# Attention batch by batch, with half steps of the feed-forward layer between its units

## The chip, the cores and the metric

The kernel runs on one core of one Trainium2 chip. The metric is the device time of one execution in microseconds; the kernel before took 638.37 us (median of 3 runs, 638.03 to 641.25). PE is TensorE, DVE VectorE, ACT ScalarE, POOL GpSimd and SP SyncE, which issues the transfers here.

## The reference, cut

Decaying linear attention over 2 batches, 8 heads, 768 tokens and head dimension 64, then two feed-forward layers over the 1536 tokens with a model dimension of 512: the first 2048 wide with a piecewise quadratic, the second 1536 wide and gated.

```python
for b in range(nb):                                   # blocks of 64 tokens
    intra = np.einsum('bhij,bhjd->bhid', np.einsum('bhic,bhjc->bhij', qb, kb) * Dmask, vb)
    inter = np.einsum('bhid,bhde->bhie', qb * lam_pow, kv_state)
    out[:, :, sl] = intra + inter
    kv_state = lam_block * kv_state + np.einsum('bhsd,bhse->bhde', kb * rev_pow, vb)
x = out.transpose(0, 2, 1, 3).reshape(B * S, H * D)
h = x @ w_in                                          # moe
x = np.where(h >= 1, h, np.where(h <= -1, 0, (h + 1) ** 2 / 4)) @ w_out
gate = 1 / (1 + np.exp(-(x @ w_gate)))                # moe2
return (gate * (x @ w_val)) @ w_out2
```

## The kernel before, in words

**Attention** goes in 16 units of 384 tokens: a batch `b`, a pair of heads `p` and a half `h` of the sequence, three chunks of 128 tokens each. The loop over `i` writes out by hand, in program order on every engine, a software pipeline: for the next unit `scores(i + 1)` and `updates(i + 1)` on PE, then `weigh_states(i + 1)` (DVE weighs the scores by the table `DT` into `pT`, L320, and adds up the states `sc`, L329 and L331; ACT copies them into the block-diagonal `st`, L343); for the unit after that `pre(i + 2)` on POOL (decayed keys `kd`, L262, and queries `qs`, L272); for this unit `outputs(i)` on PE (L354, L363) and `evacuate(i)` (ACT rounds into `xh`, L373, DVE forms the rest `xl`, L374). Then SP loads unit `i + 4` (`u_load`, four buffers) and, in most units, a piece of weights (`w_load`). The order of units is pair by pair, and within a pair batch 0 and then batch 1. The first pair's tables are made on chip; those of the other pairs go through a small tensor in DRAM (`pd`) and come back as `DT[:, 2:]` (L250) and `qp[:, 1:]` (L245). `kd` and `qs` have three buffers each.

**Weights** are float64 and come in 68 pieces of 512 columns. A weight round (`w_round`) takes three neighbouring pieces one step further each: two ACT operations take the words of piece `k` apart (`w_words`, L77, L78), two DVE operations and one on DVE or POOL make the float of piece `k - 1` (`w_float`, L84, L85, L87), ACT rounds piece `k - 2` into its high half (`w_high`, L91), and DVE or POOL forms its low half (`w_low`, L95). A piece is thus ready three rounds after its first step. Between units, rounds use POOL and stand at units 2, 4, 6, 8, 10, 12, 13, 14 and 15. There are 18 buffers for ready pieces and 6 for raw ones; a round is put off while its buffer still holds a hidden slice in use (`prog["done"]`).

**The feed-forward layers** work in steps: for a hidden slice of 128 and a token tile of 512, `hidden` (12 matmuls of 512 columns, L136 to L138; 24 in the second layer), the split of the previous step's activation into `gh` (ACT, L420) and `gl` (DVE, L421), the activation of this step, and `project` of the step before the previous one (12 matmuls, L466), a lag of two. Four slices make a group that accumulates in four PSUM banks, which `flush` adds up in SBUF. Three token tiles run inside a group. `act1` of the first layer is a relu on ACT (L428), a min and multiplication on DVE (L429), and a max on DVE (L430). One round of weights follows a step of the first layer (none behind a flush), two a step of the second. Only the very first `hidden` (`early`) is issued inside the last attention unit. PSUM is split into a pool of five banks (scores, updates, projections) and one of three (outputs, hidden).

Of the kernel before, what the change touches and what calls it, by code (L numbers as in the profile page):

```python
# [33 lines left out]
def fused_kernel(ctx: ExitStack, tc: tile.TileContext, qkv, qd, cst, w1, w2, out):  # L34
# [62 lines left out]
    # One round takes each of three pieces a step further, so that no engine waits  # L97
    # for another.
# [33 lines left out]
    def three(ps, pairs):  # L132
        """ps += A.B over pairs of split operands, without the product of the two rests."""
        n = len(pairs)
        for j, ((ah, al), (bh, bl)) in enumerate(pairs):
            pe.matmul(ps, lhsT=ah, rhs=bh, start=(j == 0), stop=False)  # L136
            pe.matmul(ps, lhsT=al, rhs=bh, start=False, stop=False)  # L137
            pe.matmul(ps, lhsT=ah, rhs=bl, start=False, stop=(j == n - 1))  # L138

    def hidden(n, t, o):  # L140
        w_need(n, o)
        ps = ps_h.tile([P, TT], F32, tag="h", name=f"h{n}_{t}_{o}")
        tt = slice(t * TT, (t + 1) * TT)
        three(ps, [(w_at(n, o + k * P), (xh[:, k, tt], xl[:, k, tt])) for k in range(NP)])
        return ps

    first = []

    def early():
        first.append(hidden(0, 0, 0))  # L150

# [1 line left out]
    with ExitStack() as actx:  # L153
# [5 lines left out]
        units = [(b, p, h) for p in range(NP) for b in range(B) for h in range(NHALF)]  # L159
# [24 lines left out]
        pw = kp.tile([H, 2 * P], F32, name="pw")  # L184
        pd = dp.tile([H, 2 * P], F32, name="pd")

        # States of a pair's heads, and the same as diagonal blocks
# [3 lines left out]
        def tables():  # L191
            # The first pair's, by doubling from the anti-diagonal.
# [19 lines left out]
            for j in range(2):  # L212
                dve.memset(dm[j][:, :, 0:PADW], 0.0)
            pool.memset(pw[:, 0:P - 1], 0.0)
# [20 lines left out]
            # The others by way of DRAM, from the powers: column x of pw holds lam^(x - 127), or 0.  # L235
# [22 lines left out]
        def pre_k(i):  # L258
            """Keys by what is left of their decay at the chunk's end."""
            b, p, h = units[i]  # L260
            kd[i] = sp2.tile([P, CU, 2, D], F32, tag="kd", bufs=3, name=f"kd{i}")
            pool.tensor_tensor(  # L262
                out=kd[i], in0=raw_u[i][:, 2].rearrange("p (c h d) -> p c h d", c=CU, h=2),
                in1=DT[:, 2 * p:2 * p + 2, P - 1:P].unsqueeze(1).to_broadcast([P, CU, 2, D]),
                op=ALU.mult,
            )

        def pre_q(i):
            """Queries by the decay since the chunk's start."""
            b, p, h = units[i]  # L270
            qs[i] = sp2.tile([P, CU, P], F32, tag="qs", bufs=3, name=f"qs{i}")
# [9 lines left out]
        def scores(i):  # L281
            u = raw_u[i]
            S_ps[i] = []
            for e in range(2):
                s = ps_a.tile([P, 512], F32, tag="a", name=f"s{i}_{e}")
                S_ps[i].append(s)
# [25 lines left out]
        def weigh_states(i):  # L312
# [3 lines left out]
            sb, sd = sc[(p * B + b) % 2], st[(p * B + b) % 2]  # L316
# [28 lines left out]
        def outputs(i):  # L345
            b, p, h = units[i]
            u = raw_u.pop(i)
            sb = st[(p * B + b) % 2]
            xb = ps_h.tile([P, TT], F32, tag="h", name=f"x{i}")
            x = xb[:, 0:UT]  # L350
# [28 lines left out]
        with tc.manual_schedule():  # L379
# [8 lines left out]
            pre_q(1)  # L388
            for i in range(nu):
# [5 lines left out]
                else:  # L395
                    early()
# [16 lines left out]
    acp = ctx.enter_context(tc.tile_pool(name="acp", bufs=1, reuse_waits="tile"))  # L413
    gp = ctx.enter_context(tc.tile_pool(name="gp", bufs=2, reuse_waits="tile"))
    part = acp.tile([P, NTT * 4, 512], F32, name="part")

    def parts(g, n, t):
        gh = gp.tile([P, TT], F32R, tag="gh", bufs=3, name=f"gh{n}_{t}")
        gl = gp.tile([P, TT], F32R, tag="gl", bufs=3, name=f"gl{n}_{t}")
        act.activation(gh, g, AF.Copy)  # L420
        dve.tensor_tensor(out=gl, in0=g, in1=gh.bitcast(F32), op=ALU.subtract)  # L421
        return gh, gl

    def act1(ps, n, t):
        """(h + 1)^2 / 4 between -1 and 1, 0 below, h above."""
        r = gp.tile([P, TT], F32, tag="r", name=f"r{n}_{t}")
        g = gp.tile([P, TT], F32, tag="g", name=f"g{n}_{t}")
        act.activation(r, ps, AF.Relu, bias=half, scale=0.5)  # L428
        dve.scalar_tensor_tensor(out=r, in0=r, scalar=1.0, in1=r, op0=ALU.min, op1=ALU.mult)  # L429
        dve.tensor_tensor(out=g, in0=r, in1=ps, op=ALU.max)  # L430
        return g

    def act2(ps, pv, n, t):
        r = gp.tile([P, TT], F32, tag="r", name=f"r{n}_{t}")
        g = gp.tile([P, TT], F32, tag="g", name=f"g{n}_{t}")
        act.activation(r, ps, AF.Sigmoid)  # L436
        dve.tensor_tensor(out=g, in0=r, in1=pv, op=ALU.mult)  # L437
        return g

    half = acp.tile([P, 1], F32, name="half")  # L440
    seq = []
    for ph, nf in ((0, NF1), (1, NF2)):
        for g in range(nf // GF):
            for t in range(NTT):
                for f in range(GF):
                    seq.append((ph, g, t, f))

    accs = {}

    def project(u, gs):  # L450
        ph, g, t, f = u
        gh, gl = gs
        n = ph * NF1 + g * GF + f
        o = (512, 1024)[ph]
        w_need(n, o)
        w = ws[index[n, o]]
        for j in range(4):
            if f == 0:
                accs[j] = ps_a.tile([P, 512], F32, tag="a", name=f"a{ph}_{g}_{t}_{j}")
            js = slice(j * P, (j + 1) * P)  # L460
            if ph == 0:
                ops = [(w[:, 0, js], gh), (w[:, 1, js], gh), (w[:, 0, js], gl)]
            else:
                ops = [(gh[:, js], w[:, 0]), (gh[:, js], w[:, 1]), (gl[:, js], w[:, 0])]
            for m, (a, b_) in enumerate(ops):
                pe.matmul(accs[j], lhsT=a, rhs=b_, start=(f == 0 and m == 0),  # L466
                          stop=(f == GF - 1 and m == 2))

# [122 lines left out]
```

## Time and profile before

| what | value |
|---|---|
| median of 3 runs | 638.37 us (638.03 to 641.25) |
| span of the profiled execution | 637.2 us |
| its own device time | not given apart; the span is 1.2 us under the median |
| PE, DVE, ACT, POOL busy | 97%, 61%, 40%, 10% of the span |
| mean granted TensorE clock | 0.994 |

The profile is one execution. Busy times of PE are modelled from starts, so a busy PE is one without gaps, not one at its peak. "idle before <- X" in a row is how long the engine stood before that instruction, and what released it. In the rows in order of time neighbouring instructions may overlap by some 0.1 us, since an instruction's window holds its fill and its drain.

### The profile page before, as it was taken

What the parts mean: (1) busy time and instruction counts of PE and PEld (TensorE: products, weight loads), DVE (VectorE), ACT (ScalarE), POOL (GpSimd) and SP (SyncE); (2) the same over time, 40 slices, a digit from 0 to 9 for tenths busy, and PEclk for the clock granted to TensorE, in tenths of its full rate; (3) what the DMA queues carried; (4) which work ended last, traced back from release to release, by engine and by line L of the source; (5) the groups of instructions that cost most, each with busy time, mean ns of one, the idle gap of its engine ahead of it and who ended that gap; (6) DMA issues with size and microseconds to landing.
All of it is one profiled execution on the core that took longest, in us unless ns stands there. A gap on an engine that the chain in (4) does not pass through costs nothing.

```text
span 637.2 us, 7903 instructions
## 1 busy us (share of the span) xinstructions
PE 617.9 (97%) x3072; PEld 503.8 (79%) x3072; DVE 387.1 (61%) x654; ACT 257.6 (40%) x463; POOL 63.7 (10%) x68
## 2 busy tenths in 40 slices
PE   6887899999999999999999999999999999999997
PEld 5776688888888888888888888888888888888885
DVE  4578898777777778778887721256842156313132
ACT  5356755455444434545474521245631143111110
POOL 4488760000000000000000000000000000000000
PEclk9889999999999999999999999999999999999999
DMA  7989432121123222222322400024410000001011
GB/s 235 342 311 359 136 100 98 60 74 67 67 66 100 66 66 67 68 65 67 99 67 66 133 1 0 1 72 127 132 34 0 1 0 1 1 0 67 0 67 66
DMA packets 16229, 53.37 MB, mean 84 GB/s; under 512 B 1720, under 2 KB 3648, under 8 KB 16192
## 3 DMA queue, kind: packets, MB, share of 16 engines
q1 hardware_dynamic: 16192, 52.87, 25.3%
q8 instruction: 24, 0.39, 0.3%
q14 instruction: 13, 0.11, 0.0%
HBM read 49.71 MB, written 3.15 MB: 83 GB/s over the span
## 4 chain that ended last, share of the span: by engine, by line
PE 90%; DVE 4%; ACT 2%; DMA 2%; POOL 1%; issue 1%; SPq 0%; POOLq 0%; ACTq 0%
PE a L466 37%; PE h L136 17%; PE h L138 17%; PE h L137 17%; DMA u<-in_qkv 1%; DVE wr L85 1%; PE s L290 1%; DVE pT L320 1%; PE x L354 1%; DVE wr L84 1%; PE x L363 1%; PE uu L305 1%; DVE sc L331 0%; DMA pd<-pw 0%; POOL w L95 0%
## 5 line engine op out<-in xcount | busy, mean ns | idle before, releaser
L136 PE MATMUL h<-xh,w 128*128 128x512 f32 x480 | 188.3, 392 | 0.0
L138 PE MATMUL h<-xl,w 128*128 128x512 f32 x480 | 187.5, 391 | 0.0
L137 PE MATMUL h<-xh,w 128*128 128x512 f32 x480 | 186.6, 389 | 0.0
L466 PE MATMUL a<-gh,w 128*128 128x512 f32 x384 | 120.9, 396 | 1.4 <-ACT gh L420 1.4
L437 DVE TENSOR_TENSOR g<-r,h 128x512 f32<-128x512 f32 x36 | 24.7, 687 | 150.6 <-PE h L138 150.6
L138 PEld LDWEIGHTS h<-xl,w 128*128 128x128 f32 x480 | 90.1, 188 | 20.2
L137 PEld LDWEIGHTS h<-xh,w 128*128 128x128 f32 x480 | 90.2, 188 | 19.6
L136 PEld LDWEIGHTS h<-xh,w 128*128 128x128 f32 x480 | 90.1, 188 | 19.3
L466 PE MATMUL a<-w,gh 128*128 128x512 f32 x288 | 90.3, 395 | 0.0
L466 PEld LDWEIGHTS a<-gh,w 128*128 128x128 f32 x384 | 72.0, 188 | 18.4 <-ACT gh L420 1.8
L420 ACT ACTIVATE gh<-g 128x512 fp32r<-128x512 f32 x84 | 52.5, 625 | 74.0 <-DVE g L437 62.1
L466 PE MATMUL a<-gl,w 128*128 128x512 f32 x192 | 76.1, 396 | 0.5 <-DVE gl L421 0.5
L428 ACT ACTIVATE r<-h,half 128x512 f32<-128x512 f32 x48 | 32.9, 686 | 103.5 <-PE h L138 103.5
L421 DVE TENSOR_TENSOR gl<-g,gh 128x512 fp32r<-128x512 f32 x84 | 58.6, 698 | 13.5 <-ACT gh L420 13.5
L429 DVE SCALAR_TENSOR_TENSOR r<-r 128x512 f32<-128x512 f32 x48 | 37.5, 782 | 45.6 <-ACT r L428 45.6
L466 PEld LDWEIGHTS a<-w,gh 128*128 128x128 f32 x288 | 54.1, 188 | 12.9
L436 ACT ACTIVATE r<-h 128x512 f32<-128x512 f32 x36 | 21.5, 597 | 98.0 <-PE h L138 98.0
L466 PE MATMUL a<-w,gl 128*128 128x512 f32 x144 | 57.0, 396 | 0.0
L91 ACT ACTIVATE w<-wr 128x512 fp32r<-128x512 f32 x68 | 42.6, 626 | 35.6 <-DVE wr L87 31.8
L85 DVE SCALAR_TENSOR_TENSOR wr<-raw,wr 128x512 uint32<-128x512 uint32 x68 | 50.2, 739 | 2.3
L77 ACT ACTIVATE wr<-raw 128x512 f32<-128x512 f32 x68 | 45.2, 664 | 5.7 <-POOL w L95 5.7
L78 ACT ACTIVATE wc<-raw 128x512 int32<-128x512 uint32 x68 | 44.8, 658 | 0.0
(51 smaller groups left out, 514.2 us busy)
## 6 DMA issues: line engine op xcount, KB each, us to landing
raw<-in_w SPq DMA_DIRECT2D x68, 512.0 KB, 3.6
u<-in_qkv SPq DMA_DIRECT2D x14, 768.0 KB, 5.2
out<-part SPq DMA_DIRECT2D x12, 256.0 KB, 2.0
u<-in_qkv SPq DMA_DIRECT2D x4, 192.0 KB, 5.4
u<-in_qkv SPq DMA_DIRECT2D x2, 384.0 KB, 6.4
qd<-in_qd SPq DMA_DIRECT2D x1, 384.0 KB, 5.7
DT<-pd SPq DMA_DIRECT2D x1, 384.0 KB, 6.1
qd<-in_qd SPq DMA_DIRECT2D x1, 256.0 KB, 3.9
```

The source lines that it names most:

```text
L77: act.activation(r, hi.bitcast(F32), AF.Copy, scale=2.0 ** -112)
L78: act.activation(c, lo, AF.Copy, scale=2.0 ** -29)
L85: dve.scalar_tensor_tensor(out=ru, in0=hi, scalar=0x80000000, in1=ru, op0=ALU.bitwise_and, op1=ALU.bitwise_or)
L91: act.activation(ws[i][:, 0], tmps[i][1], AF.Copy)
L136: pe.matmul(ps, lhsT=ah, rhs=bh, start=(j == 0), stop=False)
L137: pe.matmul(ps, lhsT=al, rhs=bh, start=False, stop=False)
L138: pe.matmul(ps, lhsT=ah, rhs=bl, start=False, stop=(j == n - 1))
L420: act.activation(gh, g, AF.Copy)
L421: dve.tensor_tensor(out=gl, in0=g, in1=gh.bitcast(F32), op=ALU.subtract)
L428: act.activation(r, ps, AF.Relu, bias=half, scale=0.5)
L429: dve.scalar_tensor_tensor(out=r, in0=r, scalar=1.0, in1=r, op0=ALU.min, op1=ALU.mult)
L466: pe.matmul(accs[j], lhsT=a, rhs=b_, start=(f == 0 and m == 0), stop=(f == GF - 1 and m == 2))
```

## The change

Units run batch by batch: all eight of batch 0, then all eight of batch 1. The states' buffers alternate by pair. From unit 7 on, a generator (`feed_forward`) is advanced by one *half step* at the end of each unit but unit 13: either `hidden` with the split of the previous step and the activation, or `project`. That puts hidden steps u0, u1, u2 into units 7, 8, 9, u3 into 11 and u4 (the second token tile) into 14, and projections of u0, u1, u2 into units 10, 12 and 15. The rest of the steps run behind the units as before. Rounds between units stand at 2, 4, 6 and 7 to 14; a weight load stands in every unit; the first eight pieces are ordered so that the hidden pieces of a slice come ahead of its projecting piece. All of PSUM is one pool of eight banks. `act1` squares on ACT, and one DVE operation does min and max together. There are 14 buffers of ready weights and 5 of raw ones, two of `kd` and of `qs`; the partial sums of the first token tile and the step's buffers are allocated ahead of attention.

```diff
-NWP, NRAW = 18, 6    # 512-column pieces of weights on chip: ready ones, and as they come
+FFREE = (13,)
+NWP, NRAW = 14, 5
@@
-    ps_a = ctx.enter_context(tc.tile_pool(name="ps_a", bufs=5, space=PSUM))
-    ps_h = ctx.enter_context(tc.tile_pool(name="ps_h", bufs=3, space=PSUM))
+    ps = ctx.enter_context(tc.tile_pool(name="ps", bufs=8, space=PSUM))
@@
+    pieces[:8] = sorted(pieces[:8], key=lambda no: 2 * no[0] + (3 if no[1] else 0))
@@
     def act1(h, n, t):
         r = gp.tile([P, TT], F32, tag="r", bufs=2, name=f"r{n}_{t}")
         act.activation(r, h, AF.Relu, bias=half, scale=0.5)
-        dve.scalar_tensor_tensor(out=r, in0=r, scalar=1.0, in1=r, op0=ALU.min, op1=ALU.mult)
-        dve.tensor_tensor(out=g, in0=r, in1=ps, op=ALU.max)
+        act.activation(r, r, AF.Square)
+        dve.scalar_tensor_tensor(out=r, in0=r, scalar=1.0, in1=h, op0=ALU.min, op1=ALU.max)
@@
+    def feed_forward(rounds):
...
+        for u in seq:
+            ph, g, t, f = u
+            n = ph * NF1 + g * GF + f
+            hs = [hidden(n, t, 0)] + ([hidden(n, t, 512)] if ph else [])
+            if fresh:
+                split()
+            fresh = u, (act2(*hs, n, t) if ph else act1(hs[0], n, t))
+            yield u
+            flushed = False
+            if len(behind) == LAG:
+                flushed = finish()
+                if not rounds:
+                    yield u
+            if rounds:
+                if ph:
+                    w_round()
+                    w_round()
+                elif not flushed:
+                    w_round()
@@
-        units = [(b, p, h) for p in range(NP) for b in range(B) for h in range(NHALF)]
+        units = [(b, p, h) for b in range(B) for p in range(NP) for h in range(NHALF)]
@@
-            kd[i] = sp2.tile([P, CU, 2, D], F32, tag="kd", bufs=3, name=f"kd{i}")
+            kd[i] = sp2.tile([P, CU, 2, D], F32, tag="kd", name=f"kd{i}")
@@
-            qs[i] = sp2.tile([P, CU, P], F32, tag="qs", bufs=3, name=f"qs{i}")
+            qs[i] = sp2.tile([P, CU, P], F32, tag="qs", name=f"qs{i}")
@@
-                else:
-                    early()
@@
-                if (i and i % 2 == 0) or i >= 13:
+                if (i and i % 2 == 0) or 7 <= i <= 13:
                     w_round(pool, finish)
                 else:
                     finish()
                 u_load(i + 4)
-                if i % 2 == 0 or i >= 12:
-                    w_load()
+                w_load()
+                if i >= nu // 2 - 1 and i not in FFREE:
+                    next(steps)
```

## Rows read from the trace of the kernel before

**Rows 1.** The page's first part: busy us, share of the span, instructions.

```profile
PE 617.9 (97%) x3072; PEld 503.8 (79%) x3072; DVE 387.1 (61%) x654; ACT 257.6 (40%) x463; POOL 63.7 (10%) x68
```

**Rows 2.** Busy time by stage: length, each engine's busy us (instructions), clock, DMA share, GB/s.

```profile
15.40:35.60 20.20, 18.18 (x237) 15.23 (x236) 11.59 (x31) 9.26 (x22) 11.56 (x13) 0.92 0.92 343
35.60:69.40 33.80, 28.30 (x344) 23.52 (x344) 29.18 (x63) 21.20 (x45) 28.38 (x28) 0.95 0.81 295
69.40:80.00 10.60, 8.72 (x38) 6.51 (x37) 8.81 (x12) 7.74 (x14) 7.30 (x5) 1.00 0.42 142
...
91.08:340.00 248.92, 248.92 (x1076) 201.66 (x1075) 197.00 (x318) 120.67 (x209) 3.29 (x2) 1.00 0.24 73
```

**Rows 3.** PE's waits from 12 to 95 us: total us, times, longest.

```profile
PE uu L305 <- POOL kd L262: 5.4, 3, 2.1
```

**Rows 4.** PE in order of time, single rows from 16 to 91 us.

```profile
16.26 0.57 PE L305 MATMUL uu<-u,kd 128*64 128x64 f32 x12
...
20.35 1.01 PE L290 MATMUL s<-u 64*128 64x128 f32 x12 [2.00 <-DMA u<-in_qkv]
...
37.86 0.94 PE L363 MATMUL x<-qs,st 128*128 128x128 f32 x6
...
42.14 1.50 PE L354 MATMUL x<-pT,u 128*64 128x128 f32 x12
...
46.25 0.83 PE L354 MATMUL x<-pT,u 128*64 128x128 f32 x12
...
91.08 0.40 PE L136 MATMUL h<-xh,w 128*128 128x512 f32 x1
```

**Rows 5.** DVE in order of time, units 6 to 9: start, us, instruction.

```profile
37.11 0.42 DVE L84 TENSOR_SCALAR wr<-wr 128x512 uint32<-128x512 uint32 x1
37.56 0.69 DVE L85 SCALAR_TENSOR_TENSOR wr<-raw,wr 128x512 uint32<-128x512 uint32 x1
...
38.95 0.55 DVE L320 TENSOR_TENSOR pT<-s,DT 128x384 f32<-128x384 f32 x1
...
40.01 0.59 DVE L331 SCALAR_TENSOR_TENSOR sc<-sc,qp,uu 128x64 f32<-128x64 f32 x2
41.99 0.56 DVE L374 TENSOR_TENSOR xl<-x,xh 128x384 fp32r<-128x384 f32 x1 [1.39 <-ACT xh L373]
42.46 0.55 DVE L320 TENSOR_TENSOR pT<-s,DT 128x384 f32<-128x384 f32 x1
...
43.58 0.27 DVE L331 SCALAR_TENSOR_TENSOR sc<-sc,qp,uu 128x64 f32<-128x64 f32 x1
```

**Rows 6.** ACT in order of time over the same units.

```profile
38.47 0.63 ACT L91 ACTIVATE w<-wr 128x512 fp32r<-128x512 f32 x1
...
39.58 0.65 ACT L78 ACTIVATE wc<-raw 128x512 int32<-128x512 uint32 x1
40.69 0.75 ACT L343 ACTIVATE st<-sc 64x192 f32<-64x192 f32 x2 [0.46 <-DVE sc L331]
41.46 0.49 ACT L373 ACTIVATE xh<-x 128x384 fp32r<-128x384 f32 x1
```

**Rows 7.** POOL in order of time over the same units.

```profile
38.40 1.27 POOL L87 TENSOR_TENSOR wr<-wr,wc 128x512 int32<-128x512 int32 x1 [1.70 <-DVE wr L85]
39.63 1.27 POOL L95 TENSOR_TENSOR w<-wr,w 128x512 fp32r<-128x512 f32 x1
40.86 0.84 POOL L262 TENSOR_TENSOR kd<-u,DT 128x384 f32<-128x384 f32 x1
```

**Rows 8.** The tables' transfer: its issue, its time to landing, and POOL's first reader's place.

```profile
12.29 0.60 SPq L250 DMA_DIRECT2D DT<-pd  x1
...
DMA to landing us min/median/max: 6.1/6.1/6.1
...
14.25 0.84 POOL L262 TENSOR_TENSOR kd<-u,DT 128x384 f32<-128x384 f32 x1 [0.74 <-DMA u<-in_qkv]
```

**Rows 9.** The min of `act1` by line: durations in ns (min/median/max).

```profile
L429 DVE SCALAR_TENSOR_TENSOR r<-r x48: 684/692/1789, 72.6 to 328.3; 128x512 f32<-128x512 f32 x48
```

More of the change, by code (lines that the diff above doesn't have):

```diff
@@ L130, in w_at @@
         return t[:, 0, o % 512:o % 512 + P], t[:, 1, o % 512:o % 512 + P]
[L132 to L138, printed above, removed]
     def hidden(n, t, o):
         w_need(n, o)
-        ps = ps_h.tile([P, TT], F32, tag="h", name=f"h{n}_{t}_{o}")
+        h = bank(f"h{n}_{t}_{o}")
@@ L143, in hidden @@
         tt = slice(t * TT, (t + 1) * TT)
[L144 to L150, printed above, removed]
+        for k in range(NP):
+            wh, wl = w_at(n, o + k * P)
+            pe.matmul(h, lhsT=wh, rhs=xh[:, k, tt], start=(k == 0), stop=False)
+            pe.matmul(h, lhsT=wl, rhs=xh[:, k, tt], start=False, stop=False)
+            pe.matmul(h, lhsT=wh, rhs=xl[:, k, tt], start=False, stop=(k == NP - 1))
@@ new lines, in hidden, with parts @@
+        return h
+    half = acp.tile([P, 1], F32, name="half")
+    part = {0: acp.tile([P, 4, 512], F32, name="part0")}
+    seq = []
+    for ph, nf in ((0, NF1), (1, NF2)):
+        for g in range(nf // GF):
+            for t in range(NTT):
+                for f in range(GF):
+                    seq.append((ph, g, t, f))
+    def parts(g, n, t):
+        gh = gp.tile([P, TT], F32R, tag="gh", name=f"gh{n}_{t}")
+        gl = gp.tile([P, TT], F32R, tag="gl", name=f"gl{n}_{t}")
+        act.activation(gh, g, AF.Copy)
+        dve.tensor_tensor(out=gl, in0=g, in1=gh.bitcast(F32), op=ALU.subtract)
+        return gh, gl
@@ new lines, in fused_kernel, with project @@
+    accs = {}
+    def project(u, gs):
+        ph, g, t, f = u
+        gh, gl = gs
+        n = ph * NF1 + g * GF + f
+        o = (512, 1024)[ph]
+        w_need(n, o)
+        w = ws[index[n, o]]
+        for j in range(4):
+            if f == 0:
+                accs[j] = bank(f"a{ph}_{g}_{t}_{j}")
+            js = slice(j * P, (j + 1) * P)
+            if ph == 0:
+                ops = [(w[:, 0, js], gh), (w[:, 1, js], gh), (w[:, 0, js], gl)]
+            else:
+                ops = [(gh[:, js], w[:, 0]), (gh[:, js], w[:, 1]), (gl[:, js], w[:, 0])]
+            for m, (a, b_) in enumerate(ops):
+                pe.matmul(accs[j], lhsT=a, rhs=b_, start=(f == 0 and m == 0),
+                          stop=(f == GF - 1 and m == 2))
@@ new lines, in flush @@
+    def flush(u):
+        ph, g, t, f = u
+        last = g == (NF1, NF2)[ph] // GF - 1
+        for j in range(4):
+            o = part[t][:, j]
+            if g == 0:
+                if j % 2 == 0:
+                    act.activation(o, accs[j], AF.Copy)
+                else:
+                    dve.tensor_copy(out=o, in_=accs[j])
+            else:
+                dve.tensor_tensor(out=o, in0=o, in1=accs[j], op=ALU.add)
+            if last and ph == 1:
+                r0 = t * TT + j * P
+                sp.dma_start(out=out[r0:r0 + P, :], in_=o)
+        if last and ph == 0:
+            tt = slice(t * TT, (t + 1) * TT)
+            for j in range(4):
+                o = part[t][:, j]
+                act.activation(xh[:, j, tt], o, AF.Copy)
+                dve.tensor_tensor(out=xl[:, j, tt], in0=o, in1=xh[:, j, tt].bitcast(F32),
+                                  op=ALU.subtract)
@@ new lines, in feed_forward, with split, finish @@
+    def feed_forward(rounds):
+        LAG = 2
+        behind = []
+        fresh = None
+        def split():
+            (ph, g, t, f), a = fresh
+            behind.append((fresh[0], parts(a, ph * NF1 + g * GF + f, t)))
+        def finish():
+            (ph, g, t, f), gs = behind.pop(0)
+            project((ph, g, t, f), gs)
+            if f == GF - 1:
+                flush((ph, g, t, f))
+            if t == NTT - 1:
+                prog["done"] += 1
+            return f == GF - 1
+        for u in seq:
+            ph, g, t, f = u
+            n = ph * NF1 + g * GF + f
+            hs = [hidden(n, t, 0)] + ([hidden(n, t, 512)] if ph else [])
[14 more added lines that the diff above has]
+                    w_round()
+        split()
+        while behind:
+            finish()
@@ L153, in fused_kernel @@
+    rounds = []
+    steps = feed_forward(rounds)
     with ExitStack() as actx:
@@ L213, in tables @@
                 dve.memset(dm[j][:, :, 0:PADW], 0.0)
+            dve.memset(half, 0.5)
             pool.memset(pw[:, 0:P - 1], 0.0)
@@ L440, in fused_kernel @@
[L440 to L467, printed above, removed]
@@ L533 @@
+                if i >= nu // 2 - 1 and i not in FFREE:
+                    next(steps)
+    late = ctx.enter_context(tc.tile_pool(name="late", bufs=1, reuse_waits="tile"))
+    for t in range(1, NTT):
+        part[t] = late.tile([P, 4, 512], F32, name=f"part{t}")
+    rounds.append(1)
+    with tc.manual_schedule():
+        for _ in steps:
+            pass
 def kernel(**inputs):
```

99 lines of the change are left out of this document (19 added, 80 removed).

## The prediction

> **What bounds the kernel now.** I read the page's busy shares first, then the busy time by stage, then PE's waits, then the instructions in order of time on each engine through two attention units. PE is busy 97% of a 637.2 us span [rows 1]. By stage that splits in two [rows 2]: from 91.08 us on PE has no idle time at all at clock 1.00, one 512-column matmul every 248.92/1076 = 0.231 us, so twelve of them (a *half step*: one `hidden` or one `project` of the first layer) take 2.78 us. Before that it is not full: 5.5 us idle between 35.6 and 69.4 us (28.30 of 33.80 busy, clock 0.95) and 1.9 us between 69.4 and 80. Its waits there are for POOL's decayed keys (5.4 us in three waits) [rows 3] and once for a load of `u` (2.0, at 20.35) [rows 4]. So only the attention stretch and the first 11 us behind it can be shortened; later DVE and ACT have room (197.00 and 120.67 busy of 248.92) and nothing that they save reaches the end.
>
> What paces attention is a ring of in-order queues, seen at units 7 and 8. DVE weighs the scores and updates the states (38.95 to 40.60, 1.65 us; 42.46 to 43.85, 1.39, for the second half of a sequence, which has two states) [rows 5]; only then can ACT copy the states (0.75) and only after that round `xh` (0.49) [rows 6]; only then can DVE form `xl`, having stood 1.39 us idle [rows 5], although the next unit's scores had been ready. Nothing overtakes. POOL does the same: `kd` at 40.86 comes right behind L87 and L95 of a weight round [rows 7]. PE needs 18.18/6 = 3.0 us per unit for the six units of 15.4 to 35.6 [rows 2]; I use 2.9 at full clock.
>
> **A common mark.** Before, hidden steps u0 to u4 (slices 0 to 3 of token tile 0, slice 0 of tile 1) and projections p0 to p2 (8 half steps, 96 matmuls, no DMA) and all of attention are done at 91.08, where the sixth hidden step begins [rows 4]. In the changed kernel exactly the same work is done when the loop over the units ends. Behind the mark both kernels have the same matmuls at the same pace, so the difference of the two times is the difference of the marks. I build the second mark on the first kernel's clock.
>
> **Unit order.** Units 2 and 3 are now the second head pair, whose tables come by way of DRAM. That transfer is issued at 12.29 and takes 6.1 us: 18.4 [rows 8]. `kd` of unit 2, at 14.25 before [rows 8], then ends at 18.4 + 0.84 = 19.2, and PE's updates, which stood at 16.26 [rows 4], with `outputs(1)` queued behind them, wait about 3 us. Of this, the 2.0 us that PE waited for `u` at 20.35 [rows 4] is given back. I take +1.5 us, the 1 us that is left and half a us for the slower clock behind the longer stop; ends 0 (the load of unit 3 and the low clock hide it) and +4 (nothing hides it, and the load of unit 5, which SP issues behind `outputs(1)`, is late too). SP now issues a weight piece in every unit, two more of 0.5 MB in the first five. At the 343 GB/s of this stretch [rows 2] that is 1.5 us each, ahead of the loads of units 6 and 8; inside the same 0 to 4.
>
> **Unit 7 and u0.** PE is through `outputs(7)` at 38.80 [rows 4], now 40.3. The low half of the first weight piece leaves POOL (L95) at 40.90 [rows 7], now 42.4, and the last three matmuls need `xl` of unit 7, 42.55 [rows 5], now 44.05. So u0 ends at about 45.3, PE having stood some 2 us.
>
> **Units 8 and 9: the main term.** The half step puts into ACT's queue, behind the weight round of the unit, `gh` of the previous step, the relu and the new square, and into DVE's queue `gl` and the min/max; the next unit's weighing stands behind that min/max. u2 runs in unit 9 and needs piece (2, 0); eleven rounds stand at units 2, 4, 6 and 7 to 14, three rounds make a piece, and this one becomes ready in the round of unit 9 itself, its low half last on POOL. So u2 waits for this chain, which begins with the min/max of u0. That ends at 45.3 + 0.2 (matmul drain) + 0.65 + 0.63 + 0.69 = 47.5, relu and square taken as ACT's 128x512 rows of 0.65 and 0.63 [rows 6], the min/max as the median of L429 [rows 9]. Then: weighing of unit 9 1.39 and states 0.75 + 0.1 of hand-over, `xh` 0.49, the round's three ACT operations 1.76 (38.47 to 40.23 [rows 6]), `gh` 0.6, relu 0.65, square 0.63, min/max of u1 0.75, weighing of unit 10 1.65, the round's two DVE operations 37.11 to 38.25 = 1.14 [rows 5], L87 0.15 + 1.25, L95 1.27 [rows 7]: 12.6. Low half of (2, 0): 60.1. PE reaches u2 at 45.3 + 2.9 + 2.8 (u1) + 2.9 = 53.9 and stands 6 us, with scores(11) and all later matmuls queued behind it.
>
> The min/max replaces two DVE operations. L429 reads `r` twice and took 0.692 us, but up to 1.789 beside POOL [rows 9]; the new form reads one operand from PSUM like L374, which stays at 0.56 [rows 5]. I take 0.69; with 1.79 twice the chain is 2.2 longer. By the Trainium skill (SBUF — State Buffer, "Who interferes with whom") a DVE instruction with at most one SBUF input does not contend with GpSimd; that sides with 0.69, and by it the 2.2 drop out. No row here has this very form.
>
> After a stop PE comes back slow: behind the wait before 41.75 the same twelve matmuls took 1.50 us instead of 0.83 [rows 4]. For 512 columns no row shows it; ends 0 and 2 us for each of the two long stops, I take 1.3 in all. By the Trainium skill (TensorE: Matmul & The Clock Gate, "Part 1: The HAM clock gate") the idle array falls to half its clock until activity releases it; that speaks against a change that makes PE stand, and by it the upper end would be nearer. u2 ends at 60.1 + 11 x 0.231 + 1.3 = 63.9.
>
> **Unit 11: u3.** Piece (3, 0) too is finished in its own unit. From 63.9: min/max +2.2, weighing of unit 11 +1.4, then PE sets the pace: unit 10 and p0, 2.9 + 2.8 = 5.7, scores(12) +0.8, weighing 1.65, two DVE operations 1.14, L87 and L95 2.67: +11.9, while PE is there at +8.6 and stands 3.3. u3 ends at 63.9 + 11.9 + 2.5 = 78.3. `qs` has two buffers now, so POOL's `qs(i+2)` waits for `outputs(i)` with L87 and L95 behind it; in units 9 and 11 DVE's two operations come later still, so it adds nothing, 0 to 1.
>
> **Rest.** Units 12 to 15 without one scores and updates 10.4, u4 2.8, p1 and p2 5.6: 18.8. From p0 on four of the eight PSUM banks belong to the projection, and four serve five tiles a unit: `outputs(12)` waits for the min/max of u3, 1 us, `outputs(14)` for `xl` of unit 13, 0.5. That is +20.0 with losses (ends 18.8 and 21): mark at 98.3. Against 91.08: +7.2.
>
> **Costed at nothing.** Behind the mark: the max that DVE loses and the square that ACT gains (48 each, 0.6 to 0.7 us), under a PE without gaps [rows 2]; with that cover gone, some 0.6 a step. Fourteen buffers: a group of the second layer holds 12 pieces, so two are ready ahead. Counting rounds, the tightest piece is the value part of a group's fourth slice, made at the end of the step before its use, in the second and the third group: two rounds' DVE operations after a step's 24 hidden matmuls, against 12 projecting and 12 gate matmuls, 2 x 2.78 = 5.6 us, before it is read; its last operation is some 2.6 us in. If that were to fail, 2 to 3 us twice.
>
> Sum: the profiled span of 637.2 (the median is 638.4, 1.2 around it) + 7.2 + 1.2 = 645.6 us. With all low ends (-1.5 order, -1.3 clock, -1.2 banks) 641.6, with the high ones (+2.5, +2.7, +2.2 contention, +1 banks) 654.
>
> **Rivals.** *The gaps are filled*: the rounds of units 9 and 11 come in time because ACT and DVE slip into PE's 5.7 us unit, and PE no longer stands from unit 7 on. It gains 5.5 + 1.9 idle and 5% of 28.30 = 1.4 of clock [rows 2], less 1.5 for the tables: 638.4 - 7.3 = 631. For it: before, POOL was late only where a weight round stood between two short units. Against it: ACT, DVE and POOL together need 12.6 us from one min/max to the piece. It decides at the point where that chain falls below PE's 8.6. *A draw*: only part of the chain binds, say one of the two stops (-3 to -6) and no table delay: 638 to 641. *Starved second layer*: the forecast and two stops of 3 us: 651. *The change doesn't interleave at all*, PE working the half steps only behind attention: the filled gaps are lost, +1.5: 640, part of the draw.
>
> **How the numbers follow.** Forecast 0.58 (its own range 641.6 to 654, nearly all beyond 0.5%, some 3.2 us, which is about what a measurement can tell from no change), filled gaps 0.21, draw 0.15, starved 0.06. Slower 0.61, within 0.5% 0.18, faster 0.21. The range reaches to the filled gaps below and leaves the forecast's uppermost end out: 631.5 to 651.
>
> **What would show it.** PE idle before the second matmul of u2 and u3, released by POOL's L95, some 6 and 3 us; the mark at about 98 instead of 91; `kd` of unit 2 released by the tables near 18.4; no PE wait behind the mark. Wrong it is if the piece of u2 is ready when PE gets there, or if PE's idle time between 35 us and the mark is under 7 us.

## The result, and the profile after

The changed kernel takes 642.65 us (median of 14 runs, 640.96 to 644.29) against 638.22 (636.89 to 641.25) for the kernel before: 1.0067 times as long, 95% interval 1.0053 to 1.0081. It is slower, 3 us less so than forecast (645.6). The profiled execution spans 640.6 us where before spans 637.2. That small difference is two large ones: the mark comes 11.9 us later, at 103.01 us instead of 91.08 [rows 4], where 7.2 had been forecast; and what lies behind the mark takes 640.6 - 103.0 = 537.6 us instead of 637.2 - 91.1 = 546.1, so 8.5 us less, where nothing had been forecast.

Busy time by stage, the view of [rows 2]: length, busy us (instructions) of PE, PE's weight loads, DVE, ACT and POOL, PE's granted clock, DMA share, GB/s.

```profile
15.40:36.60 21.20, 17.84 (x236) 14.95 (x232) 12.66 (x32) 8.94 (x21) 12.10 (x14) 0.92 0.99 370
39.00:45.60 6.60, 4.57 (x15) 3.38 (x15) 4.95 (x10) 4.63 (x9) 6.08 (x5) 0.74 0.81 320
45.60:53.50 7.90, 7.90 (x88) 6.18 (x86) 4.04 (x9) 5.06 (x10) 5.57 (x6) 1.00 0.45 165
53.50:65.50 12.00, 6.72 (x22) 4.54 (x20) 5.14 (x11) 4.34 (x9) 6.05 (x6) 0.72 0.30 111
...
73.50:83.00 9.50, 5.69 (x17) 3.82 (x15) 3.86 (x4) 3.48 (x7) 4.97 (x5) 0.64 0.53 193
83.00:103.01 20.01, 18.20 (x169) 14.68 (x169) 16.86 (x29) 13.68 (x27) 10.59 (x9) 1.00 0.30 92
103.01:351.93 248.92, 248.92 (x1100) 206.19 (x1099) 161.78 (x267) 144.65 (x244) 0.00 (x0) 1.00 0.22 69
```

The first number behind each length is PE's busy time. In three stretches PE is busy for 56% to 69% only, at a clock of 0.64 to 0.74: the half steps of u0 (39 to 45.6), u2 (53.5 to 65.5) and u3 (73.5 to 83). It also stands 3.4 us in the first row (2.0 in the like row of before) and 1.8 us, at full clock, from 83 us on. The last row is as long as the last of [rows 2], 248.92 us, and PE is busy in all of it as there, at clock 1.00 as there. Yet it holds 1100 matmuls where before held 1076: 0.2263 us each, not 0.2313.

PE in order of time, single rows (start, us, instruction, in brackets the idle time before it and what ended that):

```profile
42.08 0.79 PE L148 MATMUL h<-xh,w 128*128 128x512 f32 x1 [2.03 <-POOL w L103]
...
58.67 0.79 PE L147 MATMUL h<-xh,w 128*128 128x512 f32 x1 [4.26 <-ACT w L99]
60.48 0.80 PE L148 MATMUL h<-xh,w 128*128 128x512 f32 x1 [1.01 <-POOL w L103]
61.07 0.63 PE L149 MATMUL h<-xl,w 128*128 128x512 f32 x1
61.50 0.63 PE L147 MATMUL h<-xh,w 128*128 128x512 f32 x1
61.92 0.63 PE L148 MATMUL h<-xh,w 128*128 128x512 f32 x1
...
75.47 0.55 PE L147 MATMUL h<-xh,w 128*128 128x512 f32 x1 [1.71 <-ACT w L99]
78.12 0.80 PE L148 MATMUL h<-xh,w 128*128 128x512 f32 x1 [2.10 <-POOL w L103]
...
82.91 0.94 PE L414 MATMUL s<-u 64*128 64x128 f32 x12
...
85.14 0.88 PE L477 MATMUL x<-pT,u 128*64 128x128 f32 x12 [0.91 <-DVE r L175]
...
94.47 0.88 PE L477 MATMUL x<-pT,u 128*64 128x128 f32 x12 [0.90 <-DVE xl L497]
...
103.01 0.39 PE L147 MATMUL h<-xh,w 128*128 128x512 f32 x1
```

L147 waits for the high half of a weight piece, L148 for the low half: 11.1 us of stops in all. Behind the stops of u2 and u3 the matmuls start 0.42 to 0.43 us apart (61.07, 61.50, 61.92) instead of 0.227: half the clock, 1.2 GHz instead of 2.4 (the granted clock is 0.50 from 61 to 65 us and from 79 to 82), until the half step ends.

The three engines that make the piece for u2, single rows of the same view:

```profile
54.43 0.69 DVE L175 SCALAR_TENSOR_TENSOR r<-r,h 128x512 f32<-128x512 f32 x1 [0.29 <-ACT r L174]
...
57.05 0.69 DVE L93 SCALAR_TENSOR_TENSOR wr<-raw,wr 128x512 uint32<-128x512 uint32 x1
...
57.99 0.63 ACT L99 ACTIVATE w<-wr 128x512 fp32r<-128x512 f32 x1
...
57.92 1.28 POOL L95 TENSOR_TENSOR wr<-wr,wc 128x512 int32<-128x512 int32 x1 [2.12 <-DVE wr L93]
59.15 1.27 POOL L103 TENSOR_TENSOR w<-wr,w 128x512 fp32r<-128x512 f32 x1
```

This is the chain of the prediction: the min/max of u1 (L175), the weighing behind it, DVE's two operations of the round (L93 the second), then L95 and L103 on POOL. POOL ends at 60.42 and the second matmul of u2 starts at 60.48.

### The profile page after: what moved, and what is told of

It reads as the page before. It is cut to its first block, busy times and chain, and to the rows that moved or that the text cites. A ratio compares the mean times of both kernels' runs of the same rounds, so it can differ in the third digit from the quotient of the medians.

```text
span 640.6 us, 7876 instructions
## 1 busy us (share of the span) xinstructions
PE 614.8 (96%) x3072; PEld 506.3 (79%) x3072; DVE 353.4 (55%) x610; ACT 287.3 (45%) x511; POOL 57.0 (9%) x64
## 4 chain that ended last, share of the span: by engine, by line
PE 89%; DVE 4%; ACT 3%; DMA 1%; POOL 1%; issue 1%; SPq 0%; POOLq 0%; ACTq 0%
PE a L202 35%; PE h L148 17%; PE h L149 17%; PE h L147 17%; DVE pT L444 1%; DMA DT<-pd 1%; PE x L477 1%; PE x L486 1%; POOL w L103 1%; DVE sc L455 1%; ACT st L467 1%; ACT xh L496 1%; DVE wr L93 0%; DMA pd<-pw 0%; DVE part L216 0%
## 5 line engine op out<-in xcount | busy, mean ns | idle before, releaser
L147 PE MATMUL h<-xh,w 128*128 128x512 f32 x480 | 189.5, 395 | 6.0 <-ACT w L99 6.0
L148 PE MATMUL h<-xh,w 128*128 128x512 f32 x480 | 189.8, 395 | 5.1 <-POOL w L103 5.1
L202 PE MATMUL a<-gh,w 128*128 128x512 f32 x384 | 118.4, 390 | 0.0
L148 PEld LDWEIGHTS h<-xh,w 128*128 128x128 f32 x480 | 91.6, 191 | 25.3 <-POOL w L103 6.3
L147 PEld LDWEIGHTS h<-xh,w 128*128 128x128 f32 x480 | 91.4, 190 | 25.5 <-ACT w L99 6.5
L149 PEld LDWEIGHTS h<-xl,w 128*128 128x128 f32 x480 | 91.7, 191 | 19.0
L181 DVE TENSOR_TENSOR r<-r,h 128x512 f32<-128x512 f32 x36 | 24.7, 687 | 139.1 <-PE h L149 139.1
L202 PE MATMUL a<-w,gh 128*128 128x512 f32 x288 | 88.7, 389 | 0.0
L175 DVE SCALAR_TENSOR_TENSOR r<-r,h 128x512 f32<-128x512 f32 x48 | 33.0, 687 | 93.6 <-ACT r L174 93.6
L165 ACT ACTIVATE gh<-r 128x512 fp32r<-128x512 f32 x84 | 52.6, 626 | 62.7 <-DVE r L181 55.4
L166 DVE TENSOR_TENSOR gl<-r,gh 128x512 fp32r<-128x512 f32 x84 | 58.8, 700 | 17.5 <-ACT gh L165 17.5
L93 DVE SCALAR_TENSOR_TENSOR wr<-raw,wr 128x512 uint32<-128x512 uint32 x68 | 50.9, 749 | 2.3
```

The costliest lines, as they stand in the source:

```text
L93: dve.scalar_tensor_tensor(out=ru, in0=hi, scalar=0x80000000, in1=ru, op0=ALU.bitwise_and, op1=ALU.bitwise_or)
L147: pe.matmul(h, lhsT=wh, rhs=xh[:, k, tt], start=(k == 0), stop=False)
L148: pe.matmul(h, lhsT=wl, rhs=xh[:, k, tt], start=False, stop=False)
L149: pe.matmul(h, lhsT=wh, rhs=xl[:, k, tt], start=False, stop=(k == NP - 1))
L175: dve.scalar_tensor_tensor(out=r, in0=r, scalar=1.0, in1=h, op0=ALU.min, op1=ALU.max)
```

## The experiments

Two questions were open. Why is the same stream of matmuls faster behind the mark? And is it the late weights that delay the mark? In the expectations "behind the mark" is counted to the end of the last matmul: 541.8 us before, 533.3 after; the tail of the profile adds 4.3 to both. A start is a tile's first byte within its partition, as the two programs lay it out; its remainder modulo 256 is called its phase below. w, xh and xl start at 128 modulo 256 in both kernels. gh and gl start at 160 modulo 256 in the kernel before, 32 bytes further, because the 4-byte tile `half` lies ahead of them; in the changed kernel `half` lies behind them, and they start at 128. The tiles r and g, which PE never reads, move along with gh and gl in e1, e2, e5 and e10, but not from slice to slice in e9.

The measure of pace is one row for each kernel: PE busy (and matmuls) in 140 to 600 us, where it is never idle. The kernel before, then the changed one:

```profile
140.00:600.00 460.00, 460.00 (x2000) 375.08 (x1999) 270.57 (x438) 175.02 (x300) 0.00 (x0) 1.00 0.17 52
```

```profile
140.00:600.00 460.00, 460.00 (x2031) 381.04 (x2030) 258.75 (x423) 207.01 (x352) 0.00 (x0) 1.00 0.19 58
```

460/2000 = 0.2300 us and 460/2031 = 0.2265 us; over the 2352 matmuls behind the mark that is 8.3 us of the 8.5.

**e1: the kernel before, gh and gl at a multiple of 64 bytes.**

```diff
-    half = acp.tile([P, 1], F32, name="half")
+    half = acp.tile([P, 16], F32, name="half")[:, 0:1]
```

> The kernel before with one change: half takes 64 bytes of a partition instead of 4, so that r, g, gh and gl, which are laid out behind it, start 32 bytes higher, at a multiple of 64 bytes (198848 instead of 198816 for the first). Theory 'address': a matmul that reads gh or gl from a start that is 32 bytes past a multiple of 64 is paced at 0.233 us instead of 0.227, and some of the hidden matmuls behind it too; with the shift the pace behind the mark becomes that of the changed kernel, and the time falls by the 8.5 us by which the two kernels differ behind their marks: 629.7 us (628.5 to 631). Theory 'banks' (one pool of eight PSUM banks sets the pace) and theory 'traffic' (the max that leaves VectorE sets it) both expect no change: 638.2 us (637 to 639.5), with projections still at 0.233 us.

637.68 us (635.97 to 640.55, 10 runs) against 638.77: 0.998 [0.996, 1.000].

```profile
140.00:600.00 460.00, 460.00 (x2001) 375.71 (x2001) 269.55 (x436) 174.72 (x299) 0.00 (x0) 1.00 0.16 52
```

A miss. The pace of the whole stretch is the old one.

**e2: the changed kernel, gh and gl 32 bytes higher.**

```diff
-    half = acp.tile([P, 1], F32, name="half")
+    half = gp.tile([P, 1], F32, tag="half", bufs=1, name="half")
```

> The changed kernel with one change: half is laid out in the pool gp ahead of r, gh and gl, so that these start 32 bytes higher, 32 past a multiple of 64 bytes; every other tile keeps its address. Theory 'address': the projections go from 0.227 to 0.233 us and the time rises by about 8.5 us, to 651 us (649 to 652.5). Theories 'banks' and 'traffic': 642.6 us (641 to 644), pace unchanged at 0.227.

651.14 us (650.05 to 651.68, 4 runs): 1.0176 [1.0148, 1.0204] times the kernel before, 8.5 us over the changed kernel.

```profile
140.00:600.00 460.00, 460.00 (x2000) 375.10 (x1999) 257.43 (x421) 206.34 (x351) 0.00 (x0) 1.00 0.18 58
```

The mark stays (102.84 us), the pace falls back to 2000. Since nothing but the place of these tiles differs, banks and traffic are out; since e1 failed, so is "a multiple of 64" as the condition.

**e5: the kernel before, gh and gl at a multiple of 128 bytes (0 modulo 256).**

```diff
-    half = acp.tile([P, 1], F32, name="half")
+    half = acp.tile([P, 32], F32, name="half")[:, 0:1]
```

> The kernel before with half taking 128 bytes, so that r, g, gh and gl start at a multiple of 128 bytes (gh at 207104; in e1 it was 207040, a multiple of 64 only, and the projections stayed at 0.233 us). Theory 'address, 128': the projections go to 0.227 us, the stretch behind the mark takes the 533.3 us that it takes in the changed kernel and not 541.8, and the time is 629.9 us (628.5 to 631.5). Rival 'place': the part of the memory in which gh and gl lie, or the banks of PSUM, sets the pace and the shift is no matter: 638.4 us (637 to 640).

638.79 us (636.84 to 639.34, 10 runs) against 639.13: 0.9989 [0.9975, 1.0003], no change.

```profile
140.00:600.00 460.00, 460.00 (x2002) 375.76 (x2001) 270.92 (x439) 175.22 (x300) 0.00 (x0) 1.00 0.16 52
```

A second miss. Slow were now 160, 192 and 0 modulo 256, fast was 128, which is the phase of w, xh and xl. That left "the same phase as the other operand" and "the part of the memory".

**e9: ten starts in one execution.** The kernel before, with gh and gl cut from longer buffers: each step's split takes the next start of a list, in elements of 4 bytes. `half` takes 2048 bytes, so that start 0 has the phase of w, 128.

```diff
+    STARTS = (0, 4, 8, 16, 24, 32, 64, 96, 128, 192)
+    split_done = []
...
-        gh = gp.tile([P, TT], F32R, tag="gh", bufs=3, name=f"gh{n}_{t}")
-        gl = gp.tile([P, TT], F32R, tag="gl", bufs=3, name=f"gl{n}_{t}")
+        o = STARTS[len(split_done) % len(STARTS)]
+        split_done.append(n)
+        gh = gp.tile([P, TT + 256], F32R, tag="gh", bufs=3, name=f"gh{n}_{t}")[:, o:o + TT]
+        gl = gp.tile([P, TT + 256], F32R, tag="gl", bufs=3, name=f"gl{n}_{t}")[:, o:o + TT]
...
-    half = acp.tile([P, 1], F32, name="half")
+    half = acp.tile([P, 512], F32, name="half")[:, 0:1]
```

> The kernel before with gh and gl cut from buffers that are 1024 bytes longer, so that the start of both moves from one hidden slice to the next through 0, 16, 32, 64, 96, 128, 256, 384, 512 and 768 bytes past an address that is 128 modulo 256, as the starts of w, xh and xl all are. With gh at 128 modulo 256 the changed kernel has its projections at 0.227 us; with 160 (before, e2), 192 (e1) and 0 (e5) they were at 0.233. Theory 'same phase modulo 256': the slices that start 0, 256, 512 and 768 bytes past run at 0.227 us a matmul, all others at 0.230 to 0.235. Theory 'same phase modulo 512 or more': 0 alone, or 0 and 512, are fast. Rival 'place' (the memory above address 198784, where the changed kernel has gh at 157824, or the banks): all ten at 0.233. The time is not the point; some 633 to 638 us.

PE in order of time: the first matmul of a projection (L471), and the first hidden one behind it (L136), for the starts 96, 256, 384 and 512 bytes past the common phase:

```profile
208.65 0.63 PE L471 MATMUL a<-gh,w 128*128 128x512 f32 x2
...
211.47 0.40 PE L136 MATMUL h<-xh,w 128*128 128x512 f32 x1
...
219.75 0.62 PE L471 MATMUL a<-gh,w 128*128 128x512 f32 x2
...
222.47 0.39 PE L136 MATMUL h<-xh,w 128*128 128x512 f32 x1
...
225.19 0.62 PE L471 MATMUL a<-gh,w 128*128 128x512 f32 x2
...
227.98 0.39 PE L136 MATMUL h<-xh,w 128*128 128x512 f32 x1
...
230.72 0.61 PE L471 MATMUL a<-gh,w 128*128 128x512 f32 x2
...
233.44 0.39 PE L136 MATMUL h<-xh,w 128*128 128x512 f32 x1
```

Twelve matmuls take 2.82, 2.72, 2.79 and 2.72 us. Over all 84 projections (three to five for each entry): a twelfth of the time from the start of a projection to that of the matmul behind it, medians in ns:

| bytes past the phase of w | 0 | 16 | 32 | 64 | 96 | 128 | 256 | 384 | 512 | 768 |
|---|---|---|---|---|---|---|---|---|---|---|
| first layer (gh, gl moving) | 226.7 | 231.5 | 233.6 | 230.2 | 234.6 | 232.7 | 226.7 | 232.7 | 226.7 | 226.7 |
| second layer (gh, gl stationary) | 226.7 | 226.7 | 232.8 | 233.2 | 234.0 | 233.0 | 226.7 | 233.0 | 226.7 | 226.7 |

The four starts that are a multiple of 256 bytes past the phase of w run at 226.7 ns in both layers, in the same part of the memory and the same banks as the others. The kernels above fit the table: from 140 to 335 us the matmuls that read gh or gl took 233.6 ns on average in the kernel before (32 bytes past), 230.3 in e1 (64), 232.6 in e5 (128) and 226.7 in the changed kernel (0). One execution took 634.27 us, one of the kernel before 638.53.

**e10: the kernel before, gh and gl at 128 modulo 256.** 252 bytes more for one tile:

```diff
-    half = acp.tile([P, 1], F32, name="half")
+    half = acp.tile([P, 64], F32, name="half")[:, 0:1]
```

> The kernel before with half taking 256 bytes, so that r, g, gh and gl start at 128 modulo 256, as w, xh and xl do; nothing else changes. Theory 'same phase modulo 256' (e9): all matmuls behind the mark at 0.227 us, 533.3 us behind the mark as in the changed kernel instead of 541.8, and 630.3 us (628.5 to 631.5). Rival (other things of e9 or of the changed kernel set the pace): 638.8 us (637 to 640).

630.06 us (628.32 to 630.41, 4 runs) against 637.82: 0.9867 [0.9848, 0.9885]. The span is 628.6 with the mark at 91.05, so 537.6 us behind it, 8.5 less than the kernel before; between the medians it is 7.8.

```profile
140.00:600.00 460.00, 460.00 (x2031) 380.90 (x2030) 270.54 (x439) 176.37 (x302) 0.00 (x0) 1.00 0.16 52
```

**e11: the changed kernel, everything 128 bytes higher.**

```diff
+    ahead = ctx.enter_context(tc.tile_pool(name="ahead", bufs=1)).tile([P, 32], F32, name="ahead")
+    dve.memset(ahead, 0.0)
     wp = ctx.enter_context(tc.tile_pool(name="wp", bufs=NWP))
```

> The changed kernel with 128 bytes laid out ahead of the weights, so that every tile stands 128 bytes higher: w, xh, xl, r, gh and gl all start at 0 modulo 256 instead of 128, the attention's at 32 instead of 160. Theory 'relative' (what counts is that the two operands of a matmul have the same phase): nothing changes, 533.3 us behind the mark and 642.6 us (641 to 644.5). Theory 'absolute' (128 modulo 256 is the fast phase, 0 a slow one, as for gh in e5): every matmul of the feed-forward layers goes to 0.230 to 0.233 us, 541 to 548 us behind the mark, 650 to 657 us.

642.80 us (642.13 to 643.06, 4 runs): 1.0070 [1.0055, 1.0085] times the kernel before, as the changed kernel itself.

```profile
140.00:600.00 460.00, 460.00 (x2031) 380.91 (x2030) 258.77 (x423) 207.93 (x353) 0.00 (x0) 1.00 0.18 58
```

So it is the relation that counts, not the address.

**e3: the half steps of u0 to u3, p0 and p1 one unit later.**

```diff
-FFREE = (13,)
+FFREE = (7,)
```

> The changed kernel with FFREE = (7,) instead of (13,): the half steps of u0 to u3, p0 and p1 stand one unit later each, u4 and p2 where they were; the rounds of weights are not moved. Theory 'late weights': the stops in front of the hidden steps (2.03 us before the second matmul of u0, 4.26 and 1.01 in u2, 1.71 and 2.10 in u3; 11.1 together) end in rounds that stand in the same unit or one unit ahead; with one unit more of lead those of u2 and u3 go and the half clock behind them too (24 matmuls at 0.427 instead of 0.227, 4.8 us). The mark falls from 103.0 to 91 to 95 us, and the time to 633 us (631 to 636). Rival 'order': the units batch by batch, the shorter table lead and the bank waits cost most of the 11.9 us; then the time stays within 640 to 644.

629.56 us (627.44 to 630.83, 4 runs): 0.9848 [0.9817, 0.9879]. The execution profiled is the fastest of the four; its mark is at 88.11. PE's waits up to 200 us (total, times, longest):

```profile
PE uu L429 <- POOL kd L386: 6.2, 3, 2.8
...
PE h L148 <- POOL w L103: 1.5, 1, 1.5
PE x L477 <- DVE r L175: 0.8, 1, 0.8
PE x L477 <- DVE xl L497: 0.6, 1, 0.6
```

Of 11.1 us of waits for weights 1.5 are left, and in this execution the clock is 1.00 from 15 us on (over the whole of the other three it was 0.992 to 0.994).

**e6: the rounds earlier instead.**

```diff
-                if (i and i % 2 == 0) or 7 <= i <= 13:
+                if (i and i % 2 == 0) or 5 <= i <= 12:
```

> The changed kernel with the rounds of weights in units 2, 4 and 5 to 12 instead of 2, 4, 6 and 7 to 13, the half steps as they are (the first in unit 7). Theory 'late weights': each piece is ready one unit or more ahead of its half step, as in e3; the stops of u0, u2 and u3 and the half clock behind them go, the mark comes at 89 to 94 us, and the time is 631 us (629 to 635). Rival 'GpSimd is full': in e4 rounds in consecutive units with no half steps between them put the keys (kd) late by 16.5 us; here units 5 and 6 have rounds and no half step, each pays some 1.6 us for it, and the rounds still end late: 636 to 641 us.

629.18 us (627.70 to 631.06, 4 runs): 0.9839 [0.9811, 0.9867]; the mark at 88.65, again in the fastest of the four (627.70). The waits for weights are down to 0.7 us, and the keys wait no longer than in e3 (6.0 us):

```profile
PE uu L429 <- POOL kd L386: 6.0, 3, 2.6
...
PE h L148 <- POOL w L103: 0.7, 1, 0.7
```

Two edits with nothing in common but the lead of the weights over the half steps bring the same 13 us.

**e12: both edits, that of e3 and that of e6.**

```diff
-FFREE = (13,)
+FFREE = (7,)
...
-                if (i and i % 2 == 0) or 7 <= i <= 13:
+                if (i and i % 2 == 0) or 5 <= i <= 12:
```

> The changed kernel with both repairs, the rounds of e6 and the half steps of e3: each piece is ready two units ahead. If the late weights were the whole of the loss, e3 and e6 have won it back already and nothing is left but the 1.5 us (e3) or 0.7 us (e6) that one piece still stopped the engine: 629 us (627.5 to 630). Rival (the lead still counts, since POOL is what is full from 36 to 54 us): 626 to 627.5 us.

630.36 us (629.47 to 631.73, 4 runs): 0.9884 [0.9864, 0.9904]; the mark at 90.47. More lead brings nothing more, though no wait for weights is left: the keys still cost 6.2 us.

**e7: e3 with the attention's tiles at a multiple of 128 bytes.**

```diff
-FFREE = (13,)
+FFREE = (7,)
...
-    half = acp.tile([P, 1], F32, name="half")
+    half = acp.tile([P, 32], F32, name="half")[:, 0:1]
```

> e3 (half steps one unit later) with half taking 128 bytes as well, so that the tiles of the attention (u, kd, qs, pT, st, DT), which start 32 past a multiple of 128 bytes in the changed kernel, start at a multiple of 128 as in the kernel before. Theory 'address' carried over to the float32 matmuls of the attention: 624 matmuls gain at most 3% of some 55 us, 1.5 us: 628 us (626.5 to 629.5). Rival, the rule holds for the float32r matmuls of 512 columns alone: 629.6 us as e3 (628.5 to 630.7).

629.57 us (628.40 to 630.34, 4 runs), as e3, with the mark at 90.00. The 1.5 us of the theory did not come. All tiles of the attention (but the diagonal queries of two units) have one phase among themselves in e3 as well, so what e9 and e11 show asks for no gain here.

**e4: no half steps between the units, the rounds as they are.**

```diff
-                if i >= nu // 2 - 1 and i not in FFREE:
+                if i == nu - 1:
```

> The changed kernel with no half step between the units but the first hidden unit in the last one, as the kernel before has it; the order of the units, the rounds, the one PSUM pool, the square on ScalarE and the buffers stay. Theory 'late weights' (the half steps pay for stops that they meet, the rest of the change costs about 1 us ahead of the mark and gives back 8.5 behind it): 630 us (628.5 to 633), the mark at 90 to 94 us. Rival 'order': the order of the units and the bank waits cost the 11.9 us by themselves: 640 to 643 us.

639.23 us (638.02 to 641.24, 10 runs): 1.0001 [0.9985, 1.0016], with the fast pace behind the mark, so the mark is late, at 100.65. A miss, but not for the rival's reason: nine units in a row (6 to 14) have a round on POOL, which is never idle in the stretch below (the last engine of this row of busy time), and the keys come late (PE's waits). In the changed kernel, with half steps between the same rounds, PE waits 3.0 us for keys.

```profile
54.00:69.00 15.00, 9.89 (x120) 8.04 (x116) 13.86 (x24) 10.12 (x21) 15.00 (x13) 0.89 0.72 273
```

```profile
PE uu L429 <- POOL kd L386: 16.5, 10, 3.6
```

**e8: no half steps, and the rounds where the kernel before has them.**

```diff
-                if (i and i % 2 == 0) or 7 <= i <= 13:
+                if (i and i % 2 == 0) or i >= 13:
...
-                if i >= nu // 2 - 1 and i not in FFREE:
+                if i == nu - 1:
...
                 elif not flushed:
-                    w_round()
+                    w_round(pool if n < GF and not t else dve)
```

> The changed kernel without its half steps (but the first hidden unit in the last unit) and with the rounds where the kernel before has them: even units and units 13 to 15, and the first ones of the feed-forward layer on GpSimd. What is left of the change: the order of the units, the order of the pieces, the one PSUM pool, the square on ScalarE, 14 buffers, and the addresses. Theory (these cost what stands ahead of unit 3, 1.1 us, and the addresses give back 8.5): the mark at 92 us and 630.8 us (629 to 633.5). Rival 'order' (batch by batch, or the pool, costs several us): 636 to 640 us. e4 did not tell, since its rounds in units 7 to 13 held up the keys on GpSimd.

631.80 us (631.00 to 633.75, 4 runs): 0.9883 [0.9857, 0.9910]; the mark at 92.73, 1.7 behind that of before. PE's waits of this kernel:

```profile
PE uu L429 <- POOL kd L386: 10.0, 5, 3.9
PE s L414 <- DMA qd<-in_qd: 4.9, 2, 4.1
PE s L414 <- DMA u<-in_qkv: 1.5, 4, 0.8
```

So the order of the units, the order of the pieces, the one PSUM pool, the square on ACT and the buffers cost at most some 2 us together, ahead of the mark.

**What is added up.** From the kernel before: the phase of gh and gl -8.5 behind the mark (e10; e2 the other way round). Order, pool, square and buffers: 1.7 between the medians of e8 and e10, whose intervals overlap, so it is not told from nothing. Half steps whose weights become ready in the very unit that needs them, together with the rounds that make these weights: +11 (the changed kernel against e8). The two can't be priced apart: those rounds without the half steps cost 7.4 already (e4 against e8), by another wait, that for the keys. With weights a unit ahead (e3, e6) the half steps come out 2.2 to 2.6 us faster in the medians than without (e8), and 0.5 to 0.9 us ahead of the kernel before with the phase set right (e10); the intervals overlap in both cases, so a gain from the half steps is not shown. All of e3, e6 and e10 beat both kernels.

## Why the prediction was right, and where it was not

*Slower, and by which mechanism: right.* The stops before u2 and u3 are there, 5.3 and 3.8 us for the forecast's 6 and 3.3, each in two parts, the first ended by ACT's high half, the second by POOL's low half. The second matmul of u2 starts at 60.48 us, forecast 60.1. e3 and e6 take the cause away and with it 13 us.

*Unit order and tables, +1.5: about right.* The tables landed in 4.9 us, not 6.1 [rows 8], POOL's first `kd` from them began at 17.11 and PE waited 1.96. Scores of unit 8 start at 36.56, before at 35.56: +1.0. e8 gives 1.7 (not told from nothing) for this and all else but the half steps and their rounds.

*u0, ends at 45.3: 0.8 too early.* It ended at 46.1. The stop was 2.03 us, as priced; no clock had been priced for it, and its matmuls ran at half pace until 45.

*The chain of 12.6 us from the min/max of u0 to the piece of u2: right.* 47.66 + 0.69 = 48.35 to 60.42 is 12.1. The new min/max took its 0.69 every time, also beside POOL:

```profile
engine op xcount: duration ns min/median/max, first and last start us, forms
L175 DVE SCALAR_TENSOR_TENSOR r<-r,h x48: 674/689/690, 47.7 to 335.8; 128x512 f32<-128x512 f32 x48
```

The old form, which reads r twice, had gone up to 1789 [rows 9]. The Trainium skill (SBUF — State Buffer, "Who interferes with whom") sided with 0.69, and this row agrees.

*The clock, 1.3 us for both long stops: the mis-sized term.* u2 took 65.34 - 60.48 = 4.86 us from its second matmul on and u3 82.91 - 78.12 = 4.79, against 11 x 0.227 = 2.50 each at full clock: 2.3 us a stop, 4.65 in all, over the forecast's upper end of 2 a stop; it had only a row of 128-column matmuls to go by [rows 4]. That is 3.4 of the 4.7 us by which the mark came later than the forecast 98.3; the stop of u0 and the longer chain to u3 (12.8 instead of 11.9) are most of the rest. The Trainium skill (TensorE: Matmul & The Clock Gate, "Part 1: The HAM clock gate") lets an idle array fall to half its clock; the prediction had said that by it the upper end would be nearer, and the trace agrees: the granted clock is 0.72 and 0.64 in the two stretches.

*Banks: right in place.* `outputs(12)` waited 0.91 us for the min/max of u3 (forecast 1), `outputs(14)` 0.90 for `xl` (0.5). The forecast's two waits are 1.5 us, but its sum took only 20.0 - 18.8 = 1.2 of them; they were 1.8. From u3's end to the mark it was 20.1 us, forecast 20.0.

*"Behind the mark both kernels have the same matmuls at the same pace": wrong, the step that failed.* It made the difference of the times equal to that of the marks. The matmuls are the same, but 24 more of them fit into 248.92 us. The prediction read 0.231 us for a 512-column matmul as the engine's own pace [rows 2]. That was a mean. From 140 to 335 us matmuls that read gh or gl came 233.6 ns apart, the hidden ones 229.7; in the changed kernel both are at 226.7. The trace of before shows two paces on one engine that never waits, here in the starts of twelve hidden matmuls (2.76 us), of twelve projecting ones (2.80) and of the next:

```profile
202.28 0.40 PE L136 MATMUL h<-xh,w 128*128 128x512 f32 x1
...
205.04 0.63 PE L466 MATMUL a<-gh,w 128*128 128x512 f32 x2
...
207.84 0.40 PE L136 MATMUL h<-xh,w 128*128 128x512 f32 x1
```

With that, the moved line `half = acp.tile(...)` in the two kernels, with the new place of the pool gp, was a change to ask about. The forecast's span, 637.2 + 7.2 = 644.4, was 8.5 us too long by this step and 4.7 too short at the mark, 3.8 in all; around the span lie 1.8 us in the profiled execution of the changed kernel instead of 1.2, and the median is 0.3 over it, which leaves the 3 us by which 645.6 missed 642.65. That the sum came so near is luck, since the two errors have opposite signs: had only the pace been wrong, the kernel would have come out at some 645.6 - 8.5 = 637.1 us, no slower than before, and had only the mark been wrong, at 650.3, close to the end of the range.

*Costed at nothing: right.* The square and the min/max lie under a PE without gaps, fourteen buffers starve nothing: PE has no wait behind 103 us, and PE is busy 460.00 of 460.00 in the row above. That holds for traffic too: e10 has the old VectorE work (270.54 us busy in the row, 258.77 in e11) at the same 2031 matmuls.

*The rival "gaps are filled", 631:* its condition, the pieces in time, is e3 and e6. They came to 629.4, but not by its sum: the mark moved from 91.08 to 88.1 and 88.7 in the fastest executions, to 90.0 and 90.5 in those of e7 and e12, not by 7.3 us, and the phase gave the rest. POOL is what keeps the gaps: 6 us of waits for keys in e3 and e6, 5.4 before [rows 3]. One profiled execution does not fix a mark to better than 2 us: e1, e5, e9 and e10, which have the same instructions as the kernel before up to there, have it between 89.08 and 91.53.

## What to carry to other kernels

Work put between other work should find its operands ready a full step ahead; here one unit of lead was worth 13 us, as the engine that stopped also came back at half its clock for nearly the whole half step. Before taking "same instructions, same time" as a base, compare the start-to-start times of like instructions by the tiles that they read: where the pace depends on the tile, ask where that tile starts. And when a change moves a small tile or a pool, lay out the starts of both operands of each matmul and compare them modulo 256 bytes.

## What the runs showed of the hardware that was not expected

- A 128x512 float32r matmul stream runs at 226.7 ns a matmul when the starts of moving and stationary operand differ by a multiple of 256 bytes within the partition, and at 230 to 235 ns at the other starts tried (16 to 128, 384), whichever of the two is shifted (e9). One exception: 16 bytes with the shifted operand stationary ran at 226.7. A common shift of all tiles by 128 bytes changes nothing (e11). It cost the kernel before 8.5 us of 638 behind the mark, and 252 bytes more for one tile won them back (e10).
- The hidden matmuls behind a slow projection, whose own operands all have one phase, were slowed as well: 229 to 231 ns in the first layer behind starts 16 to 96, 227.9 behind 128 and 384, 226.7 behind 0, 256, 512 and 768 (e9). Why that lingers, and what the unit of 256 bytes stands for, these runs do not show. The Trainium skill (SBUF — State Buffer, "Specifications (TRN2)") names lines of 16 bytes; crossing those would not tell starts of 64 and 128 bytes, slow here, from 256.
- The half steps behind the stops of u2 and u3 ran at half the clock (1.2 GHz instead of 2.4) to their last or last but one matmul and lost 2.3 us each, about half as much again as the stops themselves (5.3 and 3.8 us).
